# A fused attention and two mixing blocks: first-batch low parts on VectorE, and value products moved into the next pair

## The chip, the cores and the metric

The kernel runs on one core of one Trainium2 chip. The metric is the time of one execution in device microseconds (us); before the change it is 654.72, the median of three runs. PE is TensorE's matmul queue, PEld its weight loads, DVE is VectorE, ACT ScalarE, POOL GpSimd, SP the engine whose queue issues the DMAs.

## The reference

Inputs are float32: 4 batches, 8 heads, 576 positions, head size 64, so a model width of 512.

```python
# attention, per batch and head; cum is the running sum of max(s, 0)
scores = q @ k.T / 8 + min(-(cum[:, None] - cum[None, :]), 0)   # causal
attn = exp(scores - max); attn = attn / (sum(attn) + 1e-9)
x = attn @ v                       # heads side by side: (batch, 576, 512)
# first mixing block
h = gelu_tanh(x @ w_in); u, v = halves of h          # 512 each
v_n = (v - mean(v)) / sqrt(var(v) + 1e-6) * g_ln
x = x + (u * (w_sg @ v_n + b_sg[:, None])) @ w_out
# second mixing block; x_prev is x shifted by one position
k = max((mu_k * x + (1 - mu_k) * x_prev) @ w_k, 0)
out = sigmoid((mu_r * x + (1 - mu_r) * x_prev) @ w_r) * (k * k @ w_v)
```

## The kernel before, in words

**Number format.** Most matmuls run on float32r operands that are split into a high part, which is the cast of a value, and a low part, which is the value less that cast. `split_lo` (L69, instructions at L70) makes a low part with one subtraction of two SBUF tensors. A product is then three matmuls, high by high, high by low and low by high. The weights come as 64-bit words and are rebuilt in `convert` (L75) by two ACT steps (L77, L82), two DVE steps (L83, L85), an ACT cast (L88) and a split on DVE.

**Attention** is done in 16 pairs of heads, pair `pr` holding heads 2`pr` and 2`pr`+1 and each batch having four pairs. `attn_pair` (L213) is a generator. For each of its two heads it loads keys and queries (`kq`, L222), writes the rows with the running sums into `QB` and `KB` (L227, L228), casts the queries (L234: ACT for the very first head, POOL for the rest) and the keys (L235: ACT, or DVE for heads 2 and 3), copies both casts to the other half of the partitions by DMA (L236, L237), and makes two low parts, `qa` and `KB` (L239, L240). These two are on DVE for heads 0 and 2 and on POOL for all others. There are two sets of `QB` and `KB`, and a third in batch 0.

Nine steps follow (L261): four blocks of 128 queries of the first head, one step (2, 4) for the last 64 queries of both heads together, which uses the single buffer `st5`, and four blocks of the second head. A step multiplies (L257, L258), adds the mask and takes the extreme on DVE while it leaves PSUM (L284), and exponentiates on ACT with the row sums gathered in `sums` (L292). PE then turns the result, 128 keys at a time (L307, L310), and ACT or DVE copies it to `pt1` or `pt2` (L312 to L319). The last 64 keys of step (2, 4) are turned into a bank of their own, `tq` (L318), and copied by DVE (L320).

At the end of a pair the nine columns of sums are turned by PE (`rt`, L323), and DVE adds a small constant (L325) and takes reciprocals over 9 partitions of 128 (L326). A DMA writes them to `rdram` (L327), and three DMAs broadcast them into `rbs` (L330 to L332; one buffer). The value products (L345) run at once, in two parts of 256 and 320 queries, and each part is copied from PSUM to `x_t` (L348: ACT, but DVE for the first part in batch 0). The scaling `x_t = x_t * rbs` (L360) is put off: `scale_pending` is called in the next pair at step `LATE = (2, 4)`, or at the start of a mixing block that needs that pair.

**First mixing block**, `moe1` (L381), once per batch: split `xs` of the attention's result (L394, L395), value half (`v`, L416), gelu, the row's mean and variance (L423, L424 on DVE; L425, L426 on POOL), the value norm (on POOL in batch 0, L427, on DVE in the others, L428), a cast (L430) and a split (L432), the other half (`u`), the product over positions (`sg`), the gate (L468) and the output product (`o`). The second mixing block follows after all batches, from about 418 us.

**What sets the order.** `moe1` of one batch is interleaved with the attention of the next by a planner written in the kernel (L528 to L567): every `yield` carries a cost, a pair counts as 2 units with `A_COST = 21000`, and after each step of `moe1` the attention is advanced to

```python
attention_until((b + 1) * H + LEAD + RATE[b] * H * e_done / E_COST)
```

with `LEAD = 0.9`. Batch 0's attention runs alone beforehand; the steps of `prologue` (the first weights) are mixed in at points listed in `PRO` and then after each step of `moe1`. Within that order the framework's scheduler, at compile time, fills each engine's queue by priority and by when it models an instruction as ready, so a queue can hold a later step ahead of an earlier one. Each queue then runs strictly in its order, SP's queue of DMAs included. `after(x, y)` adds an order between two instructions.

Of the kernel before, what the change touches and what calls it, by code (L numbers as in the profile page):

```python
# [33 lines left out]
HB = 1  # L34
RATE = (1.1, 1, 1, 1)
# [3 lines left out]
def fused_kernel(ctx, tc, kqT, vL, s, w_in, g_ln, w_sgT, b_sg, w_out, mu_k, mu_r, w_k, w_v, w_r, out):  # L39
# [79 lines left out]
    with tc.high_priority():  # L119
# [87 lines left out]

# [3 lines left out]


    def attn_pair(b, hp):  # L213
# [3 lines left out]
        for hh in range(2):  # L217
# [16 lines left out]
            (nc.scalar.copy if hd < 1 else nc.gpsimd.tensor_copy)(qb[64:128], kq[64:128])  # L234
            (nc.vector.tensor_copy if 1 < hd < 4 else nc.scalar.copy)(ka[0:64], kq[0:64])  # L235
# [14 lines left out]
        pt1 = at.tile([P, 2, QS + P], F32, tag="pt1", name=f"pt1_{pr}", bufs=1)  # L250
# [11 lines left out]
        for hh, i in steps:  # L262
            q0 = i * P
            w = min(q0 + P, S)
            if hh == 2:
                st = st5
            elif first and hh != 1:
                st = stf[:, 64 * i * (i + 1):64 * (i + 1) * (i + 2)]
            else:
                st = at.tile([P, 640], F32, tag="st", name=f"st{pr}_{hh}_{i}", bufs=4)  # L270
# [17 lines left out]
            if hh == 2:  # L288

                pass  # L290
# [20 lines left out]
            if i == 1:  # L311
                (nc.vector.tensor_copy if first and not hh else nc.scalar.copy)(pt1[:, hh], tp[:, :QS + P])  # L312
            elif i < 4:
                (nc.vector.tensor_copy if i == 3 and pr > 5 else nc.scalar.copy)(
                    pt2[:, hh, :i + 1, q0 - QS:w - QS], tp[:, :(i + 1) * P].rearrange("p (j m) -> p j m", m=P))
# [17 lines left out]
        for r in range(2):  # L333
            q0, n = ((0, QS), (QS, S - QS))[r]
            acc = psum1.tile([P, 512], F32, tag="acc", name=f"pv{pr}_{r}", bufs=3)
            nk = 2 if r == 0 else NT
            for kk in range(nk):
                o = max(0, kk * P - q0)
                both = []
                for a in (1, 0):  # L340
                    if r == 0:
                        pt = pt1[:, a, :QS] if kk == 0 else pt1[:, a, QS:]
                    else:
                        pt = pt2[:, a, kk, o:] if kk < 4 else pt2[:, a, 3, 0:64]
                    both.append(nc.tensor.matmul(acc[64 * a:64 * a + 64, o:n], vf[:, a, kk], pt, start=(kk == 0), stop=(kk == nk - 1)))  # L345
                after(both[1], both[0])
# [541 lines left out]
```

## Time and profile before

| what | value |
|---|---|
| three runs | 654.71, 654.72 and 656.26 us; median 654.72 |
| the profiled execution | span 655.4 us from the first to the last instruction; its own time is not listed apart from the three runs |
| first matmul | 11.8 us after the start |
| first value products of the mixing block (`v`, batches 0 to 3) | about 79, 189, 276 and 347 us |
| start of the second mixing block | 418 us |
| HBM traffic | 74.46 MB read, 28.02 MB written |

The time of a run covers the same program as the span. A row of groups names the line, engine and operation, then output and inputs by the program's names, the shapes and the count; behind it stand the busy time in us, the mean duration of one in ns, and the idle time of the engine just before these instructions with what ended it. PE's busy time counts instructions whose ends are modelled, so it can hide short waits.

### The profile page before, as it was taken

The page shows a single profiled execution, that of the slowest core. Times are in us where ns is not written, and L with a number is a line of the kernel's source. Part 1 is how long each engine was busy: PE and PEld are TensorE (multiplying, and loading weights), DVE is VectorE, ACT ScalarE, POOL GpSimd, SP SyncE. Part 2 cuts the span into 40 slices and gives each one's busy share as a digit, 9 for nine tenths or more (in the row PEclk, how much of TensorE's full clock was granted, in tenths as well). Part 3 has the DMA queues.
Part 4 walks back from the last instruction along what each step waited for, and adds up shares of the span by engine and source line. Part 5 has one row for each costly group of instructions (what it writes and reads, how often), then busy time and mean ns, then how long its engine had stood idle before and what let it go on. Part 6 is the DMA issues. An engine that isn't in the chain of part 4 may idle for free.

```text
span 655.4 us, 11462 instructions
## 1 busy us (share of the span) xinstructions
PE 620.6 (95%) x3912; PEld 547.0 (83%) x3912; DVE 478.0 (73%) x990; ACT 415.2 (63%) x933; POOL 217.5 (33%) x218
## 2 busy tenths in 40 slices
PE   1779999989999999999999999999999999999997
PEld 1547777878988998978898999888888888999997
DVE  7889688995849844479732678786975869587874
ACT  4889889984748755468732665576865778553530
POOL 7265657778535577357353120000000000000000
PEclk9899999999999999999999999999999999999999
DMA  7576563454570641833403862677563693546543
GB/s 221 164 224 212 159 212 104 142 188 122 178 241 24 197 138 38 241 111 101 142 18 88 293 230 99 214 264 220 206 217 135 210 358 140 187 167 200 210 144 121
DMA packets 56458, 112.74 MB, mean 172 GB/s; under 512 B 7680, under 2 KB 20624, under 8 KB 56400
## 3 DMA queue, kind: packets, MB, share of 16 engines
q1 hardware_dynamic: 56400, 112.01, 53.3%
q8 instruction: 31, 0.51, 0.3%
q14 instruction: 27, 0.22, 0.1%
HBM read 74.46 MB, written 28.02 MB: 156 GB/s over the span
## 4 chain that ended last, share of the span: by engine, by line
PE 81%; DVE 7%; DMA 7%; issue 2%; SPq 1%; ACT 1%; DVEq 0%; ACTq 0%
PE k L376 15%; PE sg L376 9%; PE psa L786 8%; PE r L376 8%; PE o L376 7%; PE v L376 7%; PE pv L345 6%; PE u L376 5%; PE tp L310 4%; PE psb L786 4%; PE sc L257 4%; PE sc L258 3%; PE psc L786 2%; DMA rdram<-rc 2%; DMA wsr<-in_w_sgT_dram 1%
## 5 line engine op out<-in xcount | busy, mean ns | idle before, releaser
L376 PE MATMUL k<-x,wk 128*128 128x512 f32 (+1 forms) x480 | 98.9, 368 | 0.0
L376 PEld LDWEIGHTS k<-x,wk 128*128 128x128 f32 x480 | 83.6, 189 | 14.9
L292 ACT ACTIVATE st<-st,mx 128x384 f32<-128x384 f32 (+4 forms) x128 | 74.9, 588 | 8.2 <-DVE mx L284 7.5
L257 PE MATMUL sc<-ka,qa 128*128 128x512 f32 (+3 forms) x180 | 61.8, 358 | 18.4 <-DMA ka<-ka 11.8
L284 DVE CUSTOM_DVE_ANT_0 st<-sc,mask 128x512 f32<-128x512 f32 (+3 forms) x128 | 61.9, 502 | 12.6 <-PE sc L258 12.4
L376 PE MATMUL sg<-wsg,vn 128*128 128x288 f32 x448 | 63.6, 297 | 1.5 <-DVE vn L70 1.5
L376 PEld LDWEIGHTS sg<-wsg,vn 128*128 128x128 f32 x448 | 60.3, 188 | 2.4 <-DVE vn L70 1.7
L258 PE MATMUL sc<-KB,QB 128*128 128x512 f32 (+3 forms) x180 | 56.4, 335 | 0.0
L257 PEld LDWEIGHTS sc<-ka,qa 128*128 128x128 f32 x180 | 33.3, 187 | 26.3 <-issue 17.2
L310 PE MATMUL tp<-ident,st 128*128 128x128 f32 x316 | 50.3, 279 | 0.5 <-ACT st L292 0.5
L345 PE MATMUL pv<-pt,vf 128*64 128x320 f32 (+4 forms) x448 | 50.3, 364 | 0.0
L376 PE MATMUL r<-x,wr 128*128 128x512 f32 (+1 forms) x240 | 49.5, 368 | 0.0
L376 PEld LDWEIGHTS r<-x,wr 128*128 128x128 f32 x240 | 41.9, 189 | 7.5
L376 PE MATMUL v<-wv,xs 128*128 128x512 f32 x192 | 48.0, 396 | 0.0
L345 PEld LDWEIGHTS pv<-pt,vf 128*64 128x64 f32 x448 | 29.3, 136 | 19.8 <-issue 1.6
L70 POOL TENSOR_TENSOR KB<-kq,ka 64x576 fp32r<-64x576 f32 x29 | 43.1, 1485 | 6.9 <-ACT ka L235 4.9
L70 POOL TENSOR_TENSOR qa<-kq,QB 64x576 fp32r<-64x576 f32 x29 | 44.0, 1517 | 2.1
L376 PE MATMUL u<-xs,wc 128*128 128x288 f32 x288 | 41.3, 298 | 1.1 <-DVE u L512 1.1
L310 PEld LDWEIGHTS tp<-ident,st 128*128 128x128 f32 x316 | 38.4, 143 | 4.5 <-ACT st L292 0.8
L605 ACT ACTIVATE yx<-yt,mu 128x64 f32<-128x64 f32 (+4 forms) x64 | 30.5, 530 | 17.7 <-DMA yt<-ydram 17.7
L376 PE MATMUL o<-gh,wc 128*128 128x288 f32 x192 | 40.6, 297 | 0.7 <-DMA wc<-wscr 0.7
L376 PEld LDWEIGHTS v<-wv,xs 128*128 128x128 f32 x192 | 35.0, 188 | 7.3 <-issue 0.3
(191 smaller groups left out, 1435.3 us busy)
## 6 DMA issues: line engine op xcount, KB each, us to landing
wc<-wscr SPq DMA_DIRECT2D x24, 512.0 KB
kq<-in_kqT_dram SPq DMA_DIRECT2D x32, 288.0 KB
kr<-kdram SPq DMA_DIRECT2D x12, 768.0 KB
kdram<-k SPq DMA_DIRECT2D x16, 512.0 KB
yt<-ydram SPq DMA_DIRECT2D x24, 257.0 KB
vf<-in_vL_dram SPq DMA_DIRECT2D x16, 320.0 KB
ydram<-y SPq DMA_DIRECT2D x16, 288.5 KB
gt<-gdram SPq DMA_DIRECT2D x12, 384.0 KB
```

The lines of the kernel that those rows point to most:

```text
L70: eng.tensor_tensor(out=lo, in0=x, in1=f32(hi), op=ALU.subtract)
L257: nc.tensor.matmul(sc[:m, :c1 - c0], qa[:, q], ka[:, c0:c1], start=True, stop=False)
L258: nc.tensor.matmul(sc[:m, :c1 - c0], qb[:, q], kb[:, c0:c1], start=False, stop=True)
L284: mi = nc.vector.tensor_tensor_reduce(out=st[:, c0:c1], in0=sc[:, :n], in1=mk, op0=ALU.add, op1=ALU.min, scale=-SCALE, scalar=mx[:, 0:1] i ...
L292: e = nc.scalar.activation(st[:, :w], st[:, :w], AF.Exp, bias=mx[:, last:last + 1], scale=-1.0, accum_out=sm[:, i + 5 * (hh == 1):i + 5 * ...
L310: nc.tensor.transpose(tp[:, c:c + P], st[:, j * P:(j + 1) * P], ident)
L345: both.append(nc.tensor.matmul(acc[64 * a:64 * a + 64, o:n], vf[:, a, kk], pt, start=(kk == 0), stop=(kk == nk - 1)))
L376: nc.tensor.matmul(acc, a, w_, start=(i == 0), stop=(i == n - 1))
L605: i = nc.scalar.mul(t[:, s0:s1], yt[:, s0 + d:s1 + d], mu[:, r, 1, k:k + 1])
L786: nc.tensor.matmul(to[:, :HW], l, r, start=(start and i == 0), stop=(i == len(mms) - 1), skip_group_check=True)
```

## The change

- A table `PLAN` names an engine for single operations. By it all low parts of batch 0's heads (`lq0` to `lq7`, `lk0` to `lk7`) are on DVE, and so are the five value norms of batch 0 (`vn0_0` to `vn0_4`). Everything else that the helper functions place stays on the engine it had.
- The high part of the running sums is copied by DVE instead of ACT.
- The reciprocals are no longer taken from turned sums. ACT adds the constant to the sums as they lie (128 x 9), DVE takes the reciprocals into columns 576 to 584 of `st5`, and the turning of the last 64 keys, which moves from step (2, 4) to the pair's end, turns them along: they come out in partitions 64 to 72 of the copy in `pt2`, and the DMA to `rdram` starts there.
- The value products become a function `values` that is kept in `pending` and called where the scaling was called before, in the next pair; that point moves from step (2, 4) to step (1, 2). Each of their two parts leaves PSUM by one multiplication with `rbs` on DVE, in place of a copy and a later multiplication.
- `pt1` gets a second buffer, and `st` is 512 wide instead of 640.

```diff
+PLAN = {"lk0": "D", "lk1": "D", "lk2": "D", "lk3": "D", "lk4": "D", "lk5": "D", "lk6": "D", "lk7": "D", "lq0": "D", "lq1": "D", "lq2": "D", "lq3": "D", "lq4": "D", "lq5": "D", "lq6": "D", "lq7": "D", "vn0_0": "D", "vn0_1": "D", "vn0_2": "D", "vn0_3": "D", "vn0_4": "D"}
+def place(k, d):
+    return PLAN.get(k, d)
...
-        nc.scalar.copy(cr[:, 0], cum)
+        nc.vector.tensor_copy(cr[:, 0], cum)
...
+    eps = const.tile([P, 1], F32, tag="eps", name="eps")
+    nc.gpsimd.memset(eps, SUM_EPS)
...
-            lo = nc.vector if hd in (0, 2) else nc.gpsimd
-            split_lo(lo, qa[64:128], kq[64:128], qb[64:128])
-            split_lo(lo, kb[64:128], kq[0:64], ka[0:64])
+            lq = ENG[place("lq%d" % min(hd, 16), "D" if hd in (0, 2) else "P")]
+            lk = ENG[place("lk%d" % min(hd, 16), "D" if hd in (0, 2) else "P")]
+            split_lo(lq, qa[64:128], kq[64:128], qb[64:128])
+            split_lo(lk, kb[64:128], kq[0:64], ka[0:64])
...
-        pt1 = at.tile([P, 2, QS + P], F32, tag="pt1", name=f"pt1_{pr}", bufs=1)
+        pt1 = at.tile([P, 2, QS + P], F32, tag="pt1", name=f"pt1_{pr}", bufs=2)
...
-                tp4 = psum1.tile([P, 512], F32, tag="acc", name=f"tq{pr}", bufs=3)
-                nc.tensor.transpose(tp4[:, 0:P], st[:, 512:640], ident)
-                nc.scalar.copy(pt2[:, :, :4, q0 - QS:], tp.rearrange("p (j a m) -> p a j m", j=4, a=2))
-                nc.vector.tensor_copy(pt2[:, :, 3, 0:64], tp4[:, :P].rearrange("p (a m) -> p a m", a=2))
+                ECP(f"c{pr}_2_4", "A")(pt2[:, :, :4, q0 - QS:], tp.rearrange("p (j a m) -> p a j m", j=4, a=2))
             yield (i + 1) * 200
-        rt = psum1.tile([P, 512], F32, tag="acc", name=f"rt{pr}", bufs=3)
-        nc.tensor.transpose(rt[:9, :P], sm, ident)
-        rc = at.tile([9, P], F32, tag="rc", name=f"rc{pr}")
-        nc.vector.tensor_scalar_add(rc, rt[:9, :P], SUM_EPS)
-        nc.vector.reciprocal(rc, rc)
-        nc.sync.dma_start(out=rdram[pr], in_=rc)
+        nc.scalar.add(sm, sm, eps)
+        nc.vector.reciprocal(st5[:, S:S + 9], sm)
+        tp4 = psum1.tile([P, 512], F32, tag="acc", name=f"tq{pr}", bufs=3)
+        nc.tensor.transpose(tp4[:, 0:P], st5[:, 512:640], ident)
+        nc.vector.tensor_copy(pt2[:, :, 3, 0:64], tp4[:, :P].rearrange("p (a m) -> p a m", a=2))
+        nc.sync.dma_start(out=rdram[pr].rearrange("i (a m) -> i a m", a=2), in_=pt2[64:73, :, 3, 0:64])
...
-            (nc.vector.tensor_copy if first and not r else nc.scalar.copy)(x_t[:, q0:q0 + n], acc[:, :n])
-            yield 4000
-        pending.append((x_t, rbs))
+        def values():
+            for r in range(2):
...
+                nc.vector.tensor_tensor(out=x_t[:, q0:q0 + n], in0=acc[:, :n], in1=rbs[:, q0:q0 + n], op=ALU.mult)
+
+        pending.append((x_t, values))
+        yield 8000
...
             x_t, rbs = pending.pop()
-            i = nc.vector.tensor_tensor(out=x_t, in0=x_t, in1=rbs, op=ALU.mult)
-            if early is not None:
-                after(i, early)
+            rbs()
...
-            nc.gpsimd.tensor_scalar(out=v[:m, t], in0=v[:m, t], scalar1=mv[:m, t, 0:1], scalar2=rstd[:m, t:t + 1],
-                                    op0=ALU.subtract, op1=ALU.mult) if b == 0 else nc.vector.tensor_scalar(out=v[:m, t], in0=v[:m, t], scalar1=mv[:m, t, 0:1], scalar2=rstd[:m, t:t + 1],
-                                    op0=ALU.subtract, op1=ALU.mult)
+            ENG[place(f"vn{b}_{t}", "P" if b == 0 else "D")].tensor_scalar(
+                out=v[:m, t], in0=v[:m, t], scalar1=mv[:m, t, 0:1], scalar2=rstd[:m, t:t + 1], op0=ALU.subtract, op1=ALU.mult)
...
-    LATE = (2, 4)
+    LATE = (1, 2)
```

## Rows read from the trace of the kernel before

**Rows 1.** Page, first part: busy us, share of the span, instructions.

```profile
PE 620.6 (95%) x3912; PEld 547.0 (83%) x3912; DVE 478.0 (73%) x990; ACT 415.2 (63%) x933; POOL 217.5 (33%) x218
```

**Rows 2.** Windows: length, busy us (count) per engine, granted clock, DMA share, GB/s.

```profile
0.00:80.00 80.00, 55.94 (x357) 42.39 (x358) 63.94 (x162) 62.40 (x157) 45.17 (x48) 0.96 0.65 195
80.00:190.00 110.00, 105.15 (x747) 89.75 (x747) 88.64 (x217) 82.82 (x220) 77.47 (x67) 1.00 0.54 165
190.00:276.00 86.00, 85.74 (x617) 77.09 (x616) 54.50 (x148) 52.56 (x134) 47.84 (x48) 1.00 0.46 138
300.00:320.00 20.00, 18.88 (x146) 16.66 (x145) 16.84 (x46) 14.81 (x43) 10.62 (x10) 1.00 0.53 152
```

**Rows 3.** Waits of PE, 0 to 110 us: total us, times, longest us.

```profile
PE sc L257 <- DMA ka<-ka: 11.8, 1, 11.8
PE sc L257 <- DVE mx L284: 6.9, 5, 2.9
```

**Rows 4.** Groups, POOL, 0 to 80 us: busy, mean ns | idle before.

```profile
L70 POOL TENSOR_TENSOR KB<-kq,ka 64x576 fp32r<-64x576 f32 x9 | 13.7, 1524 | 1.2 <-DVE ka L235 0.4 <-ACT ka L235 0.3
L70 POOL TENSOR_TENSOR qa<-kq,QB 64x576 fp32r<-64x576 f32 x8 | 13.1, 1641 | 0.5
L234 POOL CAST QB<-kq 64x576 fp32r<-64x576 f32 x9 | 7.1, 789 | 30.0 <-DMA kq<-in_kqT_dram 22.1 <-PE sc L258 7.8
```

**Rows 5.** Groups, DVE, 0 to 80 us.

```profile
L85 DVE SCALAR_TENSOR_TENSOR syt<-syt 128x512 uint32<-128x512 uint32 x7 | 8.1, 1164 | 0.1
L360 DVE TENSOR_TENSOR xT<-xT,rb 128x576 f32<-128x576 f32 x4 | 5.6, 1391 | 0.4 <-DMA rb<-rdram 0.4
L326 DVE RECIPROCAL rc<-rc 9x128 f32<-9x128 f32 x4 | 3.7, 934 | 0.0
L284 DVE CUSTOM_DVE_ANT_0 st<-sc,mask 128x384 f32<-128x384 f32 x6 | 3.3, 550 | 0.2 <-PE sc L258 0.2
L284 DVE CUSTOM_DVE_ANT_0 st<-sc,mask 128x256 f32<-128x256 f32 x6 | 2.4, 404 | 2.7 <-PE sc L258 2.7
L235 DVE CAST ka_f<-kq 64x576 fp32r<-64x576 f32 x1 | 1.7, 1659 | 0.0
L348 DVE COPY xT<-pv 128x256 f32<-128x256 f32 x4 | 1.6, 393 | 0.0
L325 DVE TENSOR_SCALAR rc<-rt 9x128 f32<-9x128 f32 x4 | 1.1, 274 | 0.8 <-PE rt L323 0.8
L70 DVE TENSOR_TENSOR qa<-kq,QB 64x576 fp32r<-64x576 f32 x1 | 0.8, 755 | 0.0
L235 DVE CAST ka<-kq 64x576 fp32r<-64x576 f32 x1 | 0.5, 471 | 0.0
```

**Rows 6.** Groups, POOL, 80 to 190 us.

```profile
L427 POOL TENSOR_SCALAR v<-v,mv,rstd 128x512 f32<-128x512 f32 x4 | 9.1, 2272 | 0.2
```

**Rows 7.** Line 428, whole span: ns min/median/max, first and last start us.

```profile
L428 DVE TENSOR_SCALAR v<-v,mv,rstd x15: 526/544/787, 198.3 to 385.5; 128x512 f32<-128x512 f32 x12, 64x512 f32<-64x512 f32 x3
```

**Rows 8.** Groups, DVE, 420 to 560 us.

```profile
L85 DVE SCALAR_TENSOR_TENSOR ly<-ly,lz 128x512 uint32<-128x512 uint32 x4 | 2.7, 685 | 0.0
```

**Rows 9.** Groups, ACT, 80 to 190 us.

```profile
L348 ACT COPY xT<-pv 128x320 f32<-128x320 f32 x5 | 2.1, 422 | 3.7 <-PE pv L345 3.7
L348 ACT COPY xT<-pv 128x256 f32<-128x256 f32 x5 | 1.8, 367 | 0.5 <-PE pv L345 0.5
```

**Rows 10.** The chain that ended last: start us, us, what.

```profile
61.08 0.11 PE rt L323
...
188.72 8.18 PE v L376 x36
```

**Rows 11.** Groups, DVE, 80 to 190 us.

```profile
L360 DVE TENSOR_TENSOR xT<-xT,rb 128x576 f32<-128x576 f32 x5 | 5.8, 1161 | 2.6 <-ACT xT L348 2.2 <-DMA rb<-rdram 0.4
```

**Rows 12.** Waits of DVE, 0 to 420 us: total us, times, longest us.

```profile
DVE xT L360 <- DMA rb<-rdram: 9.0, 4, 3.8
```

**Rows 13.** Timeline, DVE, 313 to 314 us: start, us, instruction, idle before.

```profile
313.45 1.72 DVE L360 TENSOR_TENSOR xT<-xT,rb 128x576 f32<-128x576 f32 x1 [2.24 <-DMA rb<-rdram]
```

More of the change, by code (lines that the diff above doesn't have):

```diff
@@ L210, in fused_kernel, with ECP @@
     last_row = [None]
+    CASTS = {"A": nc.scalar.copy, "D": nc.vector.tensor_copy, "P": nc.gpsimd.tensor_copy}
+    def ECP(k, d):
+        return CASTS[place(k, d)]
+    ENG = {"D": nc.vector, "P": nc.gpsimd}
     def attn_pair(b, hp):
@@ L233, in attn_pair @@
                 qa, ka = qaf, kaf
-            (nc.scalar.copy if hd < 1 else nc.gpsimd.tensor_copy)(qb[64:128], kq[64:128])
-            (nc.vector.tensor_copy if 1 < hd < 4 else nc.scalar.copy)(ka[0:64], kq[0:64])
+            cq = CASTS[("A" if hd < 1 else "P")]
+            ck = CASTS[("D" if 1 < hd < 4 else "A")]
+            cq(qb[64:128], kq[64:128])
+            ck(ka[0:64], kq[0:64])
             nc.sync.dma_start(out=f32(qa[0:64]), in_=f32(qb[64:128]))
             nc.sync.dma_start(out=f32(ka[64:128]), in_=f32(ka[0:64]))
-            lo = nc.vector if hd in (0, 2) else nc.gpsimd
-            split_lo(lo, qa[64:128], kq[64:128], qb[64:128])
-            split_lo(lo, kb[64:128], kq[0:64], ka[0:64])
+            lq = ENG[place("lq%d" % min(hd, 16), "D" if hd in (0, 2) else "P")]
+            lk = ENG[place("lk%d" % min(hd, 16), "D" if hd in (0, 2) else "P")]
+            split_lo(lq, qa[64:128], kq[64:128], qb[64:128])
+            split_lo(lk, kb[64:128], kq[0:64], ka[0:64])
             ops.append((qa, ka, qb, kb))
@@ L311, in attn_pair @@
             if i == 1:
-                (nc.vector.tensor_copy if first and not hh else nc.scalar.copy)(pt1[:, hh], tp[:, :QS + P])
+                ECP(f"c{pr}_{hh}_1", "D" if first and not hh else "A")(pt1[:, hh], tp[:, :QS + P])
             elif i < 4:
-                (nc.vector.tensor_copy if i == 3 and pr > 5 else nc.scalar.copy)(
+                ECP(f"c{pr}_{hh}_{i}", "D" if i == 3 and pr > 5 else "A")(
                     pt2[:, hh, :i + 1, q0 - QS:w - QS], tp[:, :(i + 1) * P].rearrange("p (j m) -> p j m", m=P))
             else:
-                tp4 = psum1.tile([P, 512], F32, tag="acc", name=f"tq{pr}", bufs=3)
-                nc.tensor.transpose(tp4[:, 0:P], st[:, 512:640], ident)
-                nc.scalar.copy(pt2[:, :, :4, q0 - QS:], tp.rearrange("p (j a m) -> p a j m", j=4, a=2))
-                nc.vector.tensor_copy(pt2[:, :, 3, 0:64], tp4[:, :P].rearrange("p (a m) -> p a m", a=2))
+                ECP(f"c{pr}_2_4", "A")(pt2[:, :, :4, q0 - QS:], tp.rearrange("p (j a m) -> p a j m", j=4, a=2))
             yield (i + 1) * 200
-        rt = psum1.tile([P, 512], F32, tag="acc", name=f"rt{pr}", bufs=3)
-        nc.tensor.transpose(rt[:9, :P], sm, ident)
-        rc = at.tile([9, P], F32, tag="rc", name=f"rc{pr}")
-        nc.vector.tensor_scalar_add(rc, rt[:9, :P], SUM_EPS)
-        nc.vector.reciprocal(rc, rc)
-        nc.sync.dma_start(out=rdram[pr], in_=rc)
+        nc.scalar.add(sm, sm, eps)
[4 more added lines that the diff above has]
+        nc.sync.dma_start(out=rdram[pr].rearrange("i (a m) -> i a m", a=2), in_=pt2[64:73, :, 3, 0:64])
         rbs = at.tile([P, S], F32, tag="rb", name=f"rb{pr}", bufs=1)
@@ L332, in attn_pair @@
         nc.sync.dma_start(out=rbs[64:, 512:], in_=rq[S:S + 64].partition_broadcast(64))
[L333 to L346, printed above, removed]
-            (nc.vector.tensor_copy if first and not r else nc.scalar.copy)(x_t[:, q0:q0 + n], acc[:, :n])
-            yield 4000
-        pending.append((x_t, rbs))
+        def values():
+            for r in range(2):
+                q0, n = ((0, QS), (QS, S - QS))[r]
+                acc = psum1.tile([P, 512], F32, tag="acc", name=f"pv{pr}_{r}", bufs=3)
+                nk = 2 if r == 0 else NT
+                for kk in range(nk):
+                    o = max(0, kk * P - q0)
+                    both = []
+                    for a in (1, 0):
+                        if r == 0:
+                            pt = pt1[:, a, :QS] if kk == 0 else pt1[:, a, QS:]
+                        else:
+                            pt = pt2[:, a, kk, o:] if kk < 4 else pt2[:, a, 3, 0:64]
+                        both.append(nc.tensor.matmul(acc[64 * a:64 * a + 64, o:n], vf[:, a, kk], pt, start=(kk == 0), stop=(kk == nk - 1)))
+                    after(both[1], both[0])
+                nc.vector.tensor_tensor(out=x_t[:, q0:q0 + n], in0=acc[:, :n], in1=rbs[:, q0:q0 + n], op=ALU.mult)
+        pending.append((x_t, values))
+        yield 8000
         if pr == B * H // 2 - 1:
@@ L466, in moe1 @@
                 yield 14 * 288 * S_W
-            eng = nc.vector if b == B - 1 else nc.gpsimd
+            eng = ENG[("D" if b == B - 1 else "P")]
             eng.tensor_tensor(out=ga[:, :S], in0=ga[:, :S], in1=u[m], op=ALU.mult)
@@ L559, in fused_kernel @@
         e_done = 0.0
+        nstep = 0
         for c in moe1(b):
             e_done += c
-            attention_until((b + 1) * H + LEAD + RATE[b] * H * e_done / E_COST)
+            attention_until((b + 1) * H + LEAD + RATE[b] * H * e_done / E_COST + 0)
+            nstep += 1
             if pro is not None and next(pro, None) is None:
```

8 lines of the change are left out of this document (3 added, 5 removed).

## The prediction

> **What bounds the kernel now.** I read the engines' shares first: PE is busy 95% of the span, DVE 73%, ACT 63%, POOL 33% [rows 1]. That average hides two regimes, so the second view is the table by stage [rows 2]. From 190 to 276 us PE is busy 85.7 of 86 us: there only less matmul work, or a rare stall, can be won. From 0 to 80 us (batch 0's attention beside the first weight conversions) PE is busy 55.9 of 80 us while DVE is busy 63.9, ACT 62.4 and POOL 45.2. From 80 to 190 us (the first mixing block beside batch 1's attention) PE is busy 105.2 of 110, DVE 88.6, ACT 82.8, POOL 77.5. The third view is what PE waited for in the first 110 us [rows 3]: 11.8 us for the first head's operands, which no edit here shortens much, since that head's low parts are on DVE already; then 6.9 us for DVE to empty score banks. So time is to be had before 190 us, and DVE's queue is the place.
>
> How much there is at most: in 0 to 80 us PE idles 24.1 us, less the 11.8 at the start, 12.3. In 80 to 190 us, 747 matmuls at the pace of the next stage (617 in 86 us) would take 104.1 us: 5.9 us to win.
>
> **Part 1: low parts and value norm leave POOL.** Of batch 0's sixteen splits, four (heads 0 and 2) are on DVE and twelve on POOL, 1.52 and 1.64 us each [rows 4], some 18.9 us of POOL's 45.2. On DVE one takes 0.755 us [rows 5]: 12 x 0.755 = 9.1 us more for DVE in 0 to 80. The five value norms take 2.27 us each on POOL [rows 6] and 0.544 (median) on DVE in the later batches [rows 7]: 2.7 us more for DVE in 80 to 190, 11.4 less for POOL. The copy of the running sums adds about 0.47 us on DVE, as the clean cast [rows 5], once.
>
> What comes back: DVE instructions with two SBUF inputs stretch while POOL works. The last conversion step takes 1.164 us here [rows 5] and 0.685 after POOL has gone quiet [rows 8]; one cast takes 1.659 against 0.471 for the same shape [rows 5]. Masks out of PSUM don't stretch (0.404 and 0.550 for 256 and 384 columns). The excess in these rows is 7 x 0.479 + 1.19 = 4.5 us; POOL loses 18.9/45.2 = 42% of its work, so 1.9 us returns (ends: none, and all 4.5).
>
> For the value norm the near rows point apart. On DVE in the later batches, with POOL about half busy, it takes 0.526 to 0.787 us, 0.544 in the median [rows 7]; the cast above, also with one input and SBUF on both sides, once took 1.19 us more than it needs. I take 0.544, the same instruction's row, and keep 5 x 1.1 = 5.6 us as the upper end. The Trainium skill (SBUF — State Buffer, "Who interferes with whom") speaks for that end: an instruction of this kind in the two-port mode takes the ports shared with GpSimd as a whole, and whoever comes second is blocked for the other's full instruction. The trace agrees on the cast and shows no such block on fifteen norms.
>
> **Part 2: unturned reciprocals.** Each pair loses DVE's addition on the turned sums, 0.274, and the reciprocal over 9 x 128, 0.934 [rows 5]: 1.21 us. In their place come ACT's addition and DVE's reciprocal, both 128 x 9; no row shows either. Bounds: nothing, and 0.37 (the small ACT copy [rows 9]) or 0.934; I take 0.25 for each, nearest to the 0.274 of another instruction that is nearly all fixed cost. PE loses the turning of the sums, 0.11 us of the chain each [rows 10]: 12 pairs lie in stages where PE is full, 1.3 us. What is added is a wait: the turning of the last 64 keys moves to the pair's end and waits for the last exp, the addition and the reciprocal; behind it on PE stand the next pair's scores or a mixing product. Exposed, 16 x 0.5 = 8 us; hidden, 0. I take 0, since the values that used to stand right behind have left, and keep 8 as an end.
>
> **Part 3: values one pair later, scaled leaving PSUM.** Per pair two evictions (ACT 0.367 and 0.422 [rows 9]; the first is DVE's, 0.393, in batch 0 [rows 5]) and the scaling, 1.391 us in 0 to 80 [rows 5] and 1.161 in 80 to 190 [rows 11], become two multiplications out of PSUM, about 0.404 and 0.48 by the masks of 256 and 384 columns: 0.88. The reciprocals' trip through DRAM no longer holds DVE: it stood 9.0 us in four waits for the broadcast row [rows 12], one of them at 313 us, 2.24 us and then a stretched 1.72 us scaling [rows 13].
>
> DMAs: the same four per pair (one write, three broadcasts), the write now behind the last key copy. The value load of two pairs on waits for the later products, on SP's queue; see the rivals. At the end of batch 0's attention the last pair's products come at once but their scaling waits for the broadcast as it did.
>
> **The sum.** 0 to 80 us, DVE: away 4 x (1.21 + 1.39 + 0.39) = 12.0; added 9.1 + 0.5 + 4 x (0.88 + 0.25) = 14.1; returned 1.9: +0.2, so even. ACT loses 4 x 0.42 + the sums' copy and gains 1.0: about -1.2. POOL loses 18.9 and a head's operands are ready some 1.6 us sooner (two splits 3.1 against 1.5). With DVE even I take -1.0 (ends -6 and +4). 80 to 190 us, DVE: away 5 x (1.21 + 1.16 - 0.88) = 7.4, added 2.7 + 1.25: -3.5; ACT -5 x 0.79 + 1.25 = -2.7; POOL -11.4. Half to all of it reaches the end, as both queues are 75 to 80% full: -3.0 (ends 0 and the 5.9 above). After 190: the turned sums -1.3, the stall at 313 -1.1 (PE's idle share of 300 to 320 us is 1.12 [rows 2]; ends 0 and -3). Against: the last pair of batch 2's input is finished nearer to its use (by the planner's shares at 98.8% of the block before instead of 95.3%, some 3 us), behind it a multiplication, a cast and a POOL split of 1.5; ends 0 and +3, I take +0.5. Sum: -1.0 - 3.0 - 1.1 - 1.3 + 0.5 = -5.9 against a span of 655.4. The median of the three runs, 654.7, lies 0.7 below that span (one run lies above it), so 648.8; I say **649.0**.
>
> **Rivals.** *No gain*: before 80 us DVE gets back in splits what it loses, and 80 to 190 is paced by latencies: only the 1.3 of PE stays and a wait eats it: 654. For it: DVE's even balance; against: DVE's waits for the broadcast go in any case.
>
> *Slower, at the head of DVE's queue*: a split needs POOL's cast of the queries, and those casts stood 30.0 us in 0 to 80, 22.1 for the load of the head and 7.8 for PE to release the buffer [rows 4]. On POOL only other operands stood behind them. If the splits stand at DVE's head for half as long for six heads of nine, that is 30.0 x 6/9 x 1/2 = 10 us with masks queued behind: 648.8 + 10 = 658.8; it decides once such waits exceed 5.9 us. Against: splits come late in the compile-time order, and DVE idles 16 us of 80 that can hold some.
>
> *Slower, SP*: the value load for two pairs on waits some 7 us longer; if queue entries behind it (heads, operand copies) lose 1 us a pair that PE feels, +16 in the worst case, +8 as a price: 656.8.
>
> *Norms that block*: POOL still casts queries in 80 to 190, and each moved norm stands as the stretched cast did: 648.8 + 5.6 = 654.4, no change. The fifteen norms [rows 7] speak against it. It is the page's rule above taken in full.
>
> *More*: with POOL nearly free, half of PE's 12.3 us before 80 us goes (-6 in place of -1.0) and 80 to 190 reaches its bound (-5.9 in place of -3.0): 648.8 - 7.9 = 640.9.
>
> **How the numbers follow.** Forecast 0.57, more 0.12, no gain 0.09, norms that block 0.04, DVE's head 0.12, SP 0.06. A measurement of this kernel can tell about 0.3% (2 us) from no change. Faster: the forecast but for 0.02, and "more": 0.67. Same: no gain, norms that block, 0.01 of the forecast: 0.14. Slower: 0.18 and 0.01: 0.19. The forecast's own range is 644 to 653; reaching to both sides until a fifth is left out: 642 to 658.
>
> **What would show it.** Right: no waits of the scaling on the broadcast, no reciprocal of 9 x 128, PE still full after 190, the last conversion step below 1.0 us in the first 80, and batch 1's first value product (now at 188.7 us [rows 10]) some 4 us sooner. Wrong: DVE waiting for POOL's casts, PE waiting for the turning of the last keys, value loads that hold SP, or a gap before batch 2's value products. A first stage that grows by over 4 us would break the sum.

## The result, and the profile after

The changed kernel takes 663.9 us in the median of four runs (661.93 to 665.66), against 654.72 before: a ratio of 1.014, with a 95% interval of 1.0116 to 1.0165. It is slower, and the prediction said faster; 663.9 also lies above its range. The profiled execution took 665.66 us with a span of 663.9, to be held against the span of 655.4 of before.

The engines' shares of the changed kernel (busy us, share of the span, instructions) are to be read beside [rows 1].

```profile
PE 628.1 (95%) x3896; PEld 548.7 (83%) x3896; DVE 466.6 (70%) x1004; ACT 409.4 (62%) x920; POOL 187.2 (28%) x202
```

DVE has 11.4 us less to do than before, ACT 5.8 and POOL 30.3, and the time rose. The windows of the changed kernel, with the columns of [rows 2], show where.

```profile
0.00:80.00 80.00, 56.37 (x340) 41.30 (x340) 60.51 (x161) 57.69 (x147) 23.26 (x35) 0.89 0.65 190
80.00:190.00 110.00, 102.76 (x699) 87.79 (x699) 83.82 (x223) 81.92 (x217) 67.16 (x64) 0.97 0.52 154
190.00:276.00 86.00, 84.98 (x612) 76.80 (x611) 49.61 (x141) 47.13 (x118) 44.45 (x45) 1.00 0.48 140
```

In both of the first two stretches PE does fewer matmuls at a lower clock: 0.89 against 0.96 in 0 to 80, 0.97 against 1.00 in 80 to 190. The first product of batch 0's mixing block starts at 82.3 us instead of 78.8 (+3.5), that of batch 1's at 193.3 instead of 188.6 (+1.2 more), and from there to the end it is 470.6 instead of 466.8 (+3.8). These three make up the 8.5 us between the spans. Of the first, the larger part is busy time, at a lower clock: from 12 us to the first mixing product PE is busy 56.9 of 70.3 us at a granted clock of 0.88, before 54.5 of 66.8 us at 0.95. So 2.4 us are busy time and 1.1 us idle time.

What PE waited for from 0 to 110 us (total us, times, longest), beside [rows 3]:

```profile
PE sc L271 <- DVE KB L74: 12.1, 1, 12.1
PE sc L271 <- DVE mx L298: 7.4, 8, 2.2
PE tp L321 <- ACT st L303: 3.6, 5, 1.4
PE tp L321 <- DVE xT L356: 1.7, 1, 1.7
```

PE's waits for masks (`mx`) are more in number and shorter, not longer in sum: 7.4 us in eight here, 6.9 in five before [rows 3]. What DVE waited for in the same stretch, beside [rows 12], which cover 0 to 420 us:

```profile
DVE xT L356 <- DMA rb<-rdram: 9.2, 3, 4.3
```

The waits for the broadcast row, 9.0 us in four before, have not gone: 9.2 us in three, and all of them now lie in the first stage (up to 420 us there is no other). The last holds PSUM banks until 81.3 us, and a turning on PE waits 1.7 us for one.

DVE's own queue shows what stands ahead of the masks. These are masks (L298) and splits (L74; those from `kq` are the heads' low parts, and of these the ones of heads 0 and 2 were on DVE before too), as the timeline of the changed kernel has them (start us, duration us, instruction).

```profile
33.59 0.76 DVE L74 TENSOR_TENSOR qa<-kq,QB 64x576 fp32r<-64x576 f32 x1
34.38 0.75 DVE L74 TENSOR_TENSOR KB<-kq,ka 64x576 fp32r<-64x576 f32 x1
35.16 0.69 DVE L74 TENSOR_TENSOR wv<-syt,wv 128x512 fp32r<-128x512 f32 x1
35.77 0.68 DVE L298 CUSTOM_DVE_ANT_0 st<-sc,mask 128x512 f32<-128x512 f32 x1
...
39.07 0.75 DVE L74 TENSOR_TENSOR KB_f<-kq,ka_f 64x576 fp32r<-64x576 f32 x1
39.85 1.11 DVE L74 TENSOR_TENSOR qa_f<-kq,QB_f 64x576 fp32r<-64x576 f32 x1
40.99 0.69 DVE L298 CUSTOM_DVE_ANT_0 st<-sc,mask 128x512 f32<-128x512 f32 x1
```

And this is PE in the same stretch of the same execution, with the idle time before an instruction and what ended it.

```profile
36.52 0.39 PE L271 MATMUL sc<-ka,qa 128*128 128x256 f32 x1 [1.86 <-DVE mx L298]
...
41.75 0.44 PE L271 MATMUL sc<-ka,qa 128*128 128x384 f32 x1 [2.15 <-DVE mx L298]
44.07 0.80 PE L271 MATMUL sc<-ka,qa 128*128 128x512 f32 x1 [0.95 <-DVE mx L298]
```

Two of the heads' splits stand ahead of a mask (in the first case a weight's split, `wv`, as well), the mask keeps its score bank, and PE stands for 1.86 and 2.15 us. What such an idle stretch can be followed by is seen in finer windows of the changed kernel (length, busy us and count of PE, PEld, DVE, ACT, POOL, then clock, DMA share, GB/s).

```profile
24.00:28.00 4.00, 2.36 (x10) 1.99 (x11) 1.79 (x6) 4.00 (x11) 0.47 (x1) 0.50 0.78 206
28.00:32.00 4.00, 3.80 (x15) 3.00 (x14) 3.91 (x9) 4.00 (x13) 1.64 (x2) 0.50 0.32 76
32.00:36.00 4.00, 2.37 (x15) 1.85 (x15) 3.88 (x8) 3.29 (x10) 0.00 (x0) 0.94 0.94 289
36.00:40.00 4.00, 2.96 (x16) 2.10 (x16) 3.94 (x16) 2.65 (x6) 1.59 (x2) 1.00 0.79 238
40.00:44.00 4.00, 1.37 (x7) 0.87 (x7) 3.90 (x9) 4.00 (x11) 0.35 (x1) 0.84 0.33 86
44.00:48.00 4.00, 3.93 (x18) 2.62 (x20) 3.81 (x12) 4.00 (x13) 0.00 (x0) 0.50 0.63 195
88.00:92.00 4.00, 2.15 (x10) 1.09 (x9) 2.97 (x7) 4.00 (x14) 2.35 (x2) 0.82 0.83 225
92.00:96.00 4.00, 4.00 (x16) 3.30 (x17) 1.87 (x7) 3.31 (x8) 1.54 (x2) 0.50 0.20 73
```

In three of these places PE was busy for 2.4, 1.4 and 2.2 of 4 us, and in the window behind the granted clock is at 0.50, the lower level of 1.2 GHz. It doesn't always follow: from 32 to 36 us PE was busy for 2.4 us as well, and the window behind stands at 1.00. From 92 to 96 us PE is full at half the clock: that alone is 2 us.

The idle time at 88 to 92 us comes from other queues. PE itself waits there 1.2 us for ACT's exponentials and then 0.6 us for an operand copy of the next head. The chain of waits of the changed kernel (start us, us, what) runs through SP there:

```profile
74.51 0.23 PE sc L272
...
79.98 0.19 PE sc L272
80.22 0.58 SPq L239
80.91 0.52 SPq L249
81.52 0.54 SPq L250
82.11 0.58 SPq L207
82.75 0.43 SPq L207
83.28 0.38 SPq L258
83.75 3.78 DMA kq<-in_kqT_dram
87.56 0.70 POOL KB L74
88.26 3.39 DMA qa<-QB
91.65 0.14 issue
91.79 0.77 PE sc L271
92.56 0.43 PE sc L272
```

SP waits 0.6 us for a score product before it may overwrite the rows of the running sums (L238, L239), and behind these in its queue stand two operand copies, two weight loads, the value load and the load of the next head, issued one after the other at about 0.6 us each. (Of the 6.5 us that SP waits for score products from 60 to 96 us, the longest wait, 4.0, comes later, from 90.9 us.) The head comes 3.78 us later, its split and its copy later still, and PE's scores start at 91.8 us, at half the clock: 0.43 us for what took 0.23 at 74.5.

### The profile page after: what moved, and what is told of

Same layout as the page of the kernel before. It is cut to its first block, busy times and chain, and to the rows that moved or that the text cites. A ratio compares the mean times of both kernels' runs of the same rounds, so it can differ in the third digit from the quotient of the medians.

```text
span 663.9 us, 11405 instructions
## 1 busy us (share of the span) xinstructions
PE 628.1 (95%) x3896; PEld 548.7 (83%) x3896; DVE 466.6 (70%) x1004; ACT 409.4 (62%) x920; POOL 187.2 (28%) x202
## 4 chain that ended last, share of the span: by engine, by line
PE 80%; DVE 7%; DMA 7%; ACT 3%; issue 1%; SPq 1%; POOL 0%; DVEq 0%; ACTq 0%; POOLq 0%
PE k L383 15%; PE sg L383 8%; PE r L383 8%; PE psa L794 8%; PE v L383 7%; PE o L383 7%; PE pv L354 7%; PE u L383 6%; PE tp L321 4%; PE psb L794 4%; PE sc L271 3%; PE sc L272 3%; PE psc L794 2%; DMA kq<-in_kqT_dram 2%; DMA sraw<-in_w_in_dram 2%
## 5 line engine op out<-in xcount | busy, mean ns | idle before, releaser
L383 PE MATMUL k<-x,wk 128*128 128x512 f32 (+1 forms) x480 | 101.1, 372 | 0.0
L271 PE MATMUL sc<-ka,qa 128*128 128x512 f32 (+3 forms) x180 | 64.1, 367 | 24.6 <-DVE KB L74 12.1
L303 ACT ACTIVATE st<-st,mx 128x256 f32<-128x256 f32 (+4 forms) x128 | 74.9, 587 | 17.6 <-DVE mx L298 16.1
L298 DVE CUSTOM_DVE_ANT_0 st<-sc,mask 128x512 f32<-128x512 f32 (+3 forms) x128 | 63.2, 507 | 20.4 <-PE sc L272 11.7
L321 PE MATMUL tp<-ident,st 128*128 128x128 f32 x316 | 51.8, 287 | 5.4 <-ACT st L303 3.6
L247 POOL CAST QB<-kq 64x576 fp32r<-64x576 f32 x29 | 21.3, 735 | 90.1 <-PE sc L272 71.9
L616 DVE SCALAR_TENSOR_TENSOR yx<-yt,mu,yx 128x64 f32<-128x64 f32 (+4 forms) x64 | 31.1, 513 | 12.8 <-ACT yx L613 12.4
```

Of the source, the lines that this page charges most:

```text
L247: cq(qb[64:128], kq[64:128])
L271: nc.tensor.matmul(sc[:m, :c1 - c0], qa[:, q], ka[:, c0:c1], start=True, stop=False)
L298: mi = nc.vector.tensor_tensor_reduce(out=st[:, c0:c1], in0=sc[:, :n], in1=mk, op0=ALU.add, op1=ALU.min, scale=-SCALE, scalar=mx[:, 0:1] i ...
L303: e = nc.scalar.activation(st[:, :w], st[:, :w], AF.Exp, bias=mx[:, last:last + 1], scale=-1.0, accum_out=sm[:, i + 5 * (hh == 1):i + 5 * ...
L321: nc.tensor.transpose(tp[:, c:c + P], st[:, j * P:(j + 1) * P], ident)
L383: nc.tensor.matmul(acc, a, w_, start=(i == 0), stop=(i == n - 1))
```

## The experiments

All variants but one are written out of the changed kernel. Part 1 is the table of engines (splits, value norms), part 2 the unturned reciprocals, part 3 the values one pair later, scaled leaving PSUM. Each ratio is to the kernel before, run beside it on the same chip, with its 95% interval.

**The layout.** The change adds a tile of 128x1 for the small constant, which moves the SBUF addresses behind it. The first kernel keeps the whole change and puts the constant into a wider `mhalf`; the second is the kernel before with an unused tile of that size.

```diff
-    mhalf = const.tile([P, 1], F32, tag="mhalf", name="mhalf")
+    mh2 = const.tile([P, 2], F32, tag="mhalf", name="mhalf")
+    mhalf, eps = mh2[:, 0:1], mh2[:, 1:2]
```

```diff
+    unused = const.tile([P, 1], F32, tag="unused", name="unused")
+    nc.gpsimd.memset(unused, 0.0)
```

> The changed kernel with the new 128 x 1 constant put into the second column of mhalf's tile, so that no tile is added ahead of the others in SBUF; all else as changed. Layout theory: the added tile moved the operands of the second mixing block, and its 128x512 matmuls went from one every 226.8 ns to one every 233.3 for that. Then their median spacing is back at 227 and the time is 3.3 us below the changed kernel, 660.6. Rival (that chip or hour was slower): spacing stays at 234 and the time at 663.9.

> The kernel before with one unused 128 x 1 tile added behind mhalf, written once. Layout theory: k and r at 233 to 234 ns, 3.3 us slower than before, 658.0. Rival: 227 ns and 654.7.

Measured: 1.0082 (1.0059 to 1.0104) and 1.0068 (1.0044 to 1.0092). The groups of the page for the longest product of the second mixing block (busy us, mean ns of one), first before, then the kernel before with the unused tile, then the changed kernel, then the changed kernel without the tile:

```profile
L376 PE MATMUL k<-x,wk 128*128 128x512 f32 (+1 forms) x480 | 98.9, 368 | 0.0
```

```profile
L378 PE MATMUL k<-x,wk 128*128 128x512 f32 (+1 forms) x480 | 101.2, 372 | 0.0
```

```profile
L383 PE MATMUL k<-x,wk 128*128 128x512 f32 (+1 forms) x480 | 101.1, 372 | 0.0
```

```profile
L383 PE MATMUL k<-x,wk 128*128 128x512 f32 (+1 forms) x480 | 98.9, 368 | 0.0
```

With the tile the block's matmuls of 512 columns start 233.3 ns apart, without it 226.8 (means, stops left out), at a clock of 1.00 in all four; with those of 256 columns, which get faster, that makes 3.3 us more over the second block's two products. It is shown both ways: taken from the change, it goes; given to the kernel before, it comes. It has nothing to do with the three parts of the change. It leaves some 5 us to explain.

**Parts alone.** Part 1, part 3, the splits of part 1, its norms, part 2, and last the rewritten code with no part at all (only the second buffer of `pt1`, the narrower `st` and the helpers); this last one is called the base. All without the extra tile. In these, and wherever no part or one part is left, the copy of the running sums is on ACT as before; with two parts or three it is on DVE as changed. A part left out has the lines marked with a minus in the diff of the change put back, and `LATE` is (2, 4) without part 3; part 1 is cut by the entries of its table, for the splits alone so:

```diff
-"vn0_0": "D", "vn0_1": "D", "vn0_2": "D", "vn0_3": "D", "vn0_4": "D"}
+}
```

> The kernel before with part 1 alone: the twelve low parts and five value norms of batch 0 on DVE; reciprocals turned, values at once, scaled in the next pair at (2, 4), as before. (pt1 has two buffers and st is 512 wide, as changed.) Theory A (splits at the head of DVE's queue cost the first 80 us): first v product at 81 to 83 us instead of 78.8, time 657 to 660. Theory B (the scaled eviction waits for the broadcast on DVE and holds PSUM banks; the splits are harmless): first v at 76 to 79, time 651 to 655.

> The kernel before with part 3 alone: values in the next pair at (1, 2) and scaled leaving PSUM, reciprocals still from turned sums, low parts and norms of batch 0 on POOL. Theory B: DVE waits for the broadcast between 60 and 85 us, first v at 81 to 84 us, time 657 to 661. Theory A: first v at or before 79 us, time 651 to 655. If it lies between (the waits need the later reciprocals of part 2 as well): first v at 79 to 80 and DVE's waits for the broadcast below 5 us.

> The kernel before (pt1 with two buffers, st 512 wide) with only the twelve low parts of batch 0 on DVE. In the run with part 1 whole, the first v product came at 82.7 us (before: 78.8) and batch 1's at 203.7 (188.6). If the splits did both: 82 to 83 and over 200, time 664 to 668. If they cost the first stage alone and the norms the second: 82 to 83, then 191 to 194, time 658 to 661.

> The kernel before (pt1 with two buffers, st 512 wide) with only batch 0's five value norms on DVE, where they took 1.320 us in the run with part 1 whole and 0.536 in the changed kernel. If the norms stretch beside POOL and hold DVE's queue: first v at 78 to 79, batch 1's 196 to 200, time 662 to 667. If not: batch 1's v at 185 to 189, time 651 to 655.

> The kernel before (pt1 with two buffers, st 512 wide; the constant in mhalf's tile) with part 2 alone: reciprocals of the unturned sums, the last keys turned at the pair's end; values at once, copied and scaled as before. If the DVE work saved (1.21 to about 0.2 us a pair) counts before 190 us: 650 to 653, batch 1's v at 184 to 187. If PE's wait for the reciprocals and the later last keys cost as much: 654 to 658, with waits of PE for the copy of the last keys.

> The kernel before with only what the other single-part runs carry along: pt1 with two buffers, st 512 wide, the helper functions that name engines. Theory: none of it touches a queue, so 653.9 to 657.3 as the kernel before, first v at 78 to 79, batch 1's at 187 to 190. Rival (the compile-time order changes with any edit, and each order has its own time): 3 us or more from 655.7 to either side, in which case differences of that size between the single-part runs show nothing.

**Two parts at a time**, which completes the eight combinations, and the rewritten base with the planner's lead moved by 0.05:

```diff
-    LEAD = 0.9
+    LEAD = 0.95
```

> Parts 2 and 3 without part 1 (no split and no value norm moved; the running sums' copy on DVE stays; the small constant shares mhalf's tile, so the layout is that of before). Additive theory (each part costs what it costs alone: recip +11, deferral +2 over the rewritten base at 656.5): 669. Pay-back theory (the late turn of the last keys is only dear while the values follow it at once, and deferral takes them away): 656 to 659, batch 0's first stage ends at 79 to 80 us. Order theory (a part has no time of its own; every build is a new order of the queues, found or not): anywhere from 655 to 668.

> Parts 1 and 3 without part 2 (the turned sums' addition and reciprocal as before). Additive theory: 656.5 + 11.5 + 2 = 670. Pay-back theory, in which deferral pays for part 2 alone and the splits keep their price: 667 to 670. Order theory: anywhere from 655 to 668, without relation to the parts' single prices.

> Parts 1 and 2 without part 3 (values at once, copied and then scaled). Additive theory: 656.5 + 11.5 + 11 = 679. Pay-back theory: also 676 to 680, since nothing pays back. Order theory: no worse than a part alone, 660 to 670.

> The rewritten base with none of the three parts; only the planner's lead of the attention over the mixing work is 0.95 heads in place of 0.9, a 0.05 head shift that changes no instruction's work, only the order in which the queues are filled from the first mixing block on. Additive and pay-back theories: within 1 us of the rewritten base, 655.5 to 657.5. Order theory: several us away from it, 659 or more, with the first stage (to 78.7 us) unchanged and the loss between 80 and 350 us.

Measured, as ratios; the last two columns are from the profile, the start of batch 0's first mixing product and PE's waits for masks (`sc <- DVE mx`) between 18 and 46 us.

| parts | ratio (95%) | first stage ends, us | mask waits, us |
|---|---|---|---|
| none | 1.0022 (0.9998 to 1.0047) | 78.7 | 1.0 |
| 1: splits and norms | 1.0195 (1.0162 to 1.0228) | 82.7 | 5.8 |
| 1: splits alone | 1.0190 (1.0133 to 1.0247) | 81.1 | 3.8 |
| 1: norms alone | 1.0054 (1.0031 to 1.0077) | 77.5 | 0.9 |
| 2 | 1.0195 (1.0170 to 1.0221) | 84.7 | 0.9 |
| 3 | 1.0047 (1.0027 to 1.0068) | 81.2 | 2.6 |
| 2 and 3 | 1.0092 (1.0064 to 1.0119) | 82.3 | 0.2 |
| 1 and 3 | 1.0223 (1.0190 to 1.0256) | 84.5 | 3.5 |
| 1 and 2 | 1.0238 (1.0193 to 1.0282) | 87.2 | 3.3 |
| 1, 2 and 3 | 1.0082 (1.0059 to 1.0104) | 81.8 | 6.0 |
| none, lead 0.95 | 1.0088 (1.0060 to 1.0115) | 78.0 | 2.3 |

No combination is faster than the base, and the parts don't add: 0.0173 for part 1 and 0.0173 for part 2 over the base, 0.0216 for both, 0.0060 for all three. Of the expectations for single parts, the base's was met. With part 1 the stage ended where its first theory said (82.7 us), but the time, 668.0, was beyond both of its ranges; with part 3 alone the second theory's stage end and time were met (81.2 us, 658.4); the splits alone (668.2) lay just above the range in which they cost both stages, norms alone (658.0) between their two ranges, and part 2 alone (667.5) beyond both. Parts 1 and 2 together (671.4) lay above the order theory's range and below the two others'. The additive theory falls. Of the pay-back theory the deferral's sign holds beside part 2 (it takes 0.0103 from part 2 alone and 0.0156 from parts 1 and 2, and costs 0.0025 by itself); its number for parts 2 and 3, 656 to 659, was missed with a median of 661.3. The lead, which changes no instruction's work, costs the base 0.0066: differences of this size can come from the order of the queues alone. One row speaks against the splits as the price of the whole change: without them, with parts 2 and 3, the mask waits are nearly gone (0.2 us), and yet the first stage ends at 82.3 us and the time is no better than with all three. The first matmul comes at 10.8 us there and at 11.9 with all three, so the stage behind it takes 71.5 us without the splits and 69.9 with them.

What the order does can be read in the splits alone. Behind the first stage this kernel has the same instructions on the same engines as the base. The windows from one stage's start to the next, first the base, then the splits alone:

```profile
78.70:191.50 112.80, 108.95 (x755) 93.79 (x754) 90.79 (x219) 84.35 (x225) 80.18 (x68) 0.97 0.53 163
```

```profile
81.10:198.30 117.20, 108.59 (x746) 92.60 (x744) 85.55 (x218) 83.98 (x220) 77.44 (x65) 0.96 0.51 155
```

4.4 us more for fewer matmuls, with DVE and POOL less busy: a full queue is not what holds this stage.

**The held bank, earlier values, and the lead.** The whole change without the tile, first with only batch 0's last pair copied out of PSUM by ACT and scaled in SBUF, then with the values at step (2, 4) as the scaling was before, then with the lead at 0.95. The fourth is parts 2 and 3 with the values at step (2, 4). The expectations of the second and the fourth take this step for a later one than (1, 2). It is the other way round: of a pair's nine steps (2, 4) is the fifth and (1, 2) the eighth, so both runs call the values three steps sooner and leave the broadcast less time.

```diff
+                if first and hp == KD - 1:
+                    nc.scalar.copy(x_t[:, q0:q0 + n], acc[:, :n])
+                    nc.vector.tensor_tensor(out=x_t[:, q0:q0 + n], in0=x_t[:, q0:q0 + n], in1=rbs[:, q0:q0 + n], op=ALU.mult)
```

```diff
-    LATE = (1, 2)
+    LATE = (2, 4)
```

> All parts of the change, small constant in mhalf's tile (as in the first experiment, 660.9), but the last pair of batch 0 is copied out of PSUM by ScalarE and scaled in SBUF afterwards, so its banks don't wait for the broadcast. Held-bank theory (the bank held to 81.3 us stops PE, PE's clock falls to half at about 90 us, some 1.4 us of wait and 3.4 us of half speed): no wait of a transposition on the multiplication near 80 us, clock 0.95 or more from 80 to 100 us, 656 to 658. Order theory (this too is only another order): anywhere from 655 to 668, and the clock in 80 to 100 not tied to that wait.

> All parts, small constant in mhalf's tile, but the values of a pair come at the fifth step of the next pair, as the scaling did before, instead of the second; so the broadcast has some 3 us longer. Held-bank theory: the first two waits of the multiplication on the broadcast in the first stage (1.0 and 3.9 us) go, first stage 1 to 2 us shorter than in the first experiment, 658 to 660. Order theory: 655 to 668, without relation to these waits.

> All parts, small constant in mhalf's tile, the planner's lead 0.95 heads in place of 0.9: the same harmless step that cost the rewritten base 4.5 us. Held-bank theory: the first stage is the same, 660 to 662. Order theory: at least 2 us away from 660.9 on either side.

> Parts 2 and 3 without part 1 (661.3 in its run) with the values at the fifth step of the next pair. Held-bank theory: the one wait of the multiplication on the broadcast in the first stage (4.9 us) goes, first stage ends 1 to 3 us sooner, 656 to 659, which could reach before's time. Order theory: 655 to 668.

Measured: 1.0062 (1.0039 to 1.0085), 1.0145 (1.0110 to 1.0179), 1.0141 (1.0106 to 1.0176) and 1.0229 (1.0172 to 1.0286). The first takes the held bank away, and PE's waits in 70 to 100 us have no multiplication any more; but DVE still waits for the broadcast there, 4.3 us and 3.9 us in one wait each. PE is idle again, the clock is 0.83 from 80 to 100 us as it was, and the gain of 0.0020 lies within the intervals. So the held bank costs less than these runs can tell. With the values called sooner the first stage ends at 86.0 and 86.5 us instead of 81.8 and 82.3, and the waits for the broadcast up to 110 us are 7.1 us in each, where they were 8.7 and 4.9. What more time for the broadcast would give was not tried.

**The lead on the other side**, 0.85 in the line shown above, for the base and for the whole change without the tile.

> The rewritten base with none of the three parts, the planner's lead 0.85 heads in place of 0.9. Order theory, with the lead found by trial for this program: slower than the base's 656.5, as at 0.95 (661.0): 659 to 666. If the lead were a slope (attention sooner is worse), 652 to 655, and a version that beats before.

> All parts, small constant in mhalf's tile, the planner's lead 0.85 heads in place of 0.9. Order theory: 3 us or more away from 660.9, slower if 0.9 was found by trial for this order (663 to 670). Slope theory: 655 to 658. Held-bank theory: 660 to 662, since the first stage is the same.

Measured: 1.0026 (1.0004 to 1.0047) and 1.0107 (1.0080 to 1.0134). For the base 0.85 is as good as 0.9, so neither the slope nor a setting that loses on both sides holds; the change at 0.85 is 2.1 us from its time at 0.90, where the order theory asked for 3 or more. No version beats the kernel before. But the three leads give three pairs, base against change. Up to 74 us the order on PE, DVE, ACT and POOL is the same at all three leads, for the base and for the change, so in the first stage the pairs are one comparison made three times. Their stage starts and spans, from the profiles:

| lead | first stage, base | change | rest of the span, base | change | ratio, base | change |
|---|---|---|---|---|---|---|
| 0.85 | 75.2 | 82.9 | 576.2 | 577.6 | 1.0026 | 1.0107 |
| 0.90 | 78.7 | 81.8 | 577.2 | 578.2 | 1.0022 | 1.0082 |
| 0.95 | 78.0 | 82.9 | 582.8 | 582.5 | 1.0088 | 1.0141 |

The change costs 7.7, 3.1 and 4.9 us in the first stage, 5.2 in the mean, and +1.4, +1.0 and -0.3 us behind it, 0.7 in the mean. By the ratios it costs 0.53 to 0.81%, or 3.5 to 5.3 us. (The 7.7 is high: the base's profile at 0.85 is its fastest execution, 653.46 us against a median of 656.6.) The base's three stage ends don't overlap the change's three, so the loss of the whole change lies before the first mixing product, whatever the order behind it. PE's waits between 18 and 46 us at a lead of 0.85 show the same difference, first the base, then the change:

```profile
PE sc L269 <- DVE mx L296: 1.8, 2, 1.0
```

```profile
PE sc L271 <- DVE mx L298: 4.2, 4, 1.6
```

In all ten profiles with the splits on DVE, PE waits 2.8 to 6.3 us for masks in that stretch, and in the ten others 0.2 to 2.6. This holds for that stretch alone. Over the whole first stage the waits are 7.1, 7.0 and 5.3 us for the change in the three pairs and 2.3, 4.4 and 1.8 for the base, 3.6 more in the mean; but over all twenty profiles the two groups overlap there (3.5 to 9.0 and 1.8 to 6.9), and the kernel before, with 6.9, has as much as the change: one wait of 2.9 us at 47 us, outside the stretch, makes up the difference. Where part 2 stands without part 1, another wait takes that place: the turning of the last keys waits for the reciprocal (`tq <- DVE st`), 2.8 us with part 2 alone and 2.6 with parts 2 and 3 before 80 us.

## Why the prediction was wrong

**The loads.** Right one by one, and better in sum. A split takes 0.75 to 0.93 us on DVE by its form, 0.80 in the mean, where 0.755 was taken; the conversion 0.687 in place of 1.164 [rows 5]; the value norm 0.536; the two multiplications out of PSUM 0.424 and 0.489, where 0.404 and 0.48 were taken; ACT's addition 0.304 and the reciprocal 0.207, where 0.25 each was. The seven conversions alone gave back 3.3 us, where 1.9 was taken for everything, and DVE's busy time from 0 to 80 us fell by 3.4 us.

**The term of the first stage, -1.0 with ends of -6 and +4.** This is the step that failed: "+0.2, so even" for DVE, and from there a stage no longer than before. DVE got lighter still, and the stage grew: by 3.5 us in the profile, and by 5.2 in the mean of the three pairs. A balance of busy time is not enough here: DVE is idle a fifth of the stage and PE nearly a third [rows 2], and the stage is a string of handovers. What the trace shows is that it matters which instruction stands ahead of a mask when a score bank is full: two of the heads' splits on DVE delay a mask, and PE feels 1.9 to 2.2 us at once. The prediction's rival at the head of DVE's queue looked at the right place for a wait that didn't come: in the changed kernel no split's wait for a cast of POOL is among DVE's waits; the masks wait for the splits' own 0.75 us. That this is the price of the stage is not shown. Without the splits (parts 2 and 3) it ends no sooner, and other waits stand in the masks' place (2.6 us for the reciprocal at the turning of the last keys, 1.9 us for a low part on POOL).

**The cost that had no term: the clock.** An idle stretch of PE can be paid twice, by itself and by half a clock behind it, as from 88 to 96 us. The mean granted clock fell from 0.994 to 0.982, and of the 3.5 us of the first stage 2.4 are busy time. Of the same first stage, in the same order, the base's profile at 0.83 and 0.83 in 20 to 40 and 40 to 60 us ended it at 78.7 us, the one at 0.91 and 1.00 at 75.2.

**The term of 80 to 190 us, -3.0.** It measured +1.2. "Half to all of it reaches the end, as both queues are 75 to 80% full" is the same mistake: DVE lost 4.8 us and POOL 10.3 in that window, and nothing reached the end. At the one place followed above the way goes through SP, a head's load, its split and its copy. In the three pairs this stretch moved by -2.6, -1.7 and +5.4 us (leads of 0.85, 0.90, 0.95), so a gain or a loss of the change here isn't told apart from the order.

**The waits for the broadcast.** "The reciprocals' trip through DRAM no longer holds DVE" was wrong: 9.2 us of waits, where the first stage had 0.4 [rows 5]. The values are called at the eighth step of the next pair, three behind the scaling's, and still DVE comes to the three multiplications that wait 1.9 to 4.8 us behind the issue of the reciprocals' write, while the trip from that issue to the multiplication takes 5.8 to 7.2 us. Why the queue has them so early was not looked into. The stall at 313 us [rows 13] did go.

**The turning of the last keys, hidden at 0 with an end of 8.** Between them: 2.6 to 2.8 us in one wait wherever part 2 stands without part 1; in the changed kernel it was hidden.

**The rival on SP.** Its wait came, and its price didn't show. SP's value loads wait for value products as follows in the changed kernel, where it was 4.6 us in five waits, 1.8 the longest, before.

```profile
SPq L258 <- PE pv L354: 30.4, 9, 12.2
```

Some 24 us of it lie behind 190 us, where the time hardly moved (next paragraph); 2.8 us stand at 48 us, in the first stage. What they cost there was not tried.

**After 190 us**, -1.9 by the sum of its terms: from the start of batch 1's mixing block to the end it is 470.6 us against 466.8, and 467.1 without the extra tile, so +0.3.

**The layout**, +3.3 us, stood in no step. No row of the profile before told of it.

**Norms that block.** The value norm took 0.536 us in the changed kernel, as taken, and 1.320 in the mean with part 1 alone. There the timeline shows, on DVE and then on POOL of the same kernel:

```profile
106.06 1.73 DVE L442 TENSOR_SCALAR v<-v,mv,rstd 128x512 f32<-128x512 f32 x1 [2.29 <-POOL rstd L441]
113.30 0.54 DVE L442 TENSOR_SCALAR v<-v,mv,rstd 128x512 f32<-128x512 f32 x1
```

```profile
106.11 1.41 POOL L74 TENSOR_TENSOR KB<-kq,ka 64x576 fp32r<-64x576 f32 x1
108.59 1.64 POOL L74 TENSOR_TENSOR vn<-v,vn 128x512 fp32r<-128x512 f32 x1 [1.07 <-issue]
...
112.48 0.58 POOL L441 TENSOR_TENSOR rstd<-rstd,mhalf 128x1 f32<-128x1 f32 x1
114.60 1.29 POOL L74 TENSOR_TENSOR vn<-v,vn 128x512 fp32r<-128x512 f32 x1 [1.55 <-ACT vn L444]
```

The norm that meets a split on POOL ends 0.3 us behind that split, and the one that falls between two takes 0.54. The Trainium skill (SBUF — State Buffer, "Who interferes with whom") describes this, for an instruction in the two-port mode, as one engine being blocked for the other's full instruction. This trace agrees with the block; which of the two came first it doesn't settle, as the norm starts 0.05 us ahead of the split and is the one that is stretched. Which of the two a norm gets differs from build to build: the means in three others are 0.541, 0.594 and 0.770 us.

**What stays open.** That the whole change loses its time by the layout and before the first mixing product is shown; which waits make up the loss there is not. Why the splits cost 11 us without part 2 (1.0195 against 1.0022, 1.0223 against 1.0047) and none beside parts 2 and 3 (1.0092 without, 1.0082 with) isn't settled. The runs show that another order of the queues behind the first stage moves the time by itself, by up to 4 us for the lead; that it explains the whole of those 11 us was not shown. Nor was a kernel tried in which the order is held fixed while the engine of the splits changes, or one in which the values come later than at the eighth step.

## What to carry to other kernels

Where PE is idle for want of handovers, look at what stands behind a moved instruction in the new queue, as well as at the busy time that it adds: here the busy times of DVE, ACT and POOL all fell and the stage grew. Allow for the half clock that can follow an idle stretch. Measure a change beside a few versions that differ only in order (here a lead of 0.85, 0.90 and 0.95), and compare pairs: a single build can be off by 4 us by its order alone. Before naming a cause, take it out of the whole change too, and not only put it into the kernel before. Put new small constants into a tile that exists, and look at the pace of matmuls that the change doesn't touch before explaining anything else.

## What was not expected of the hardware

A tile of four bytes in each partition that no instruction reads slowed 128x512 matmuls far away by 3%, from 226.8 to 233.3 ns from one start to the next, and sped up those of 256 columns, from 119.9 to 116.7. Which address rule lies behind it was not tried.
